# kv and kv Wo on TensorE: 32-column tiles in one batch, or 64-column tiles and four full matmuls

## The chip, the cores and the metric

The kernel runs on one core of one Trainium2 chip. The metric is the device time of one execution in microseconds. The kernel before took a median of 164.47 us over three runs (164.33 to 164.56).

## The reference, cut to what matters

The output mixes two branches of the same input `x` (2048 x 512, bf16), row by row, with a gate `g`:

```python
x = A_x
g = _sigmoid((x * gate_w).sum(-1, keepdims=True))
a = _A_ref(x, A_wqkv, A_wo)                 # linear attention, 32 heads of 16
b = _B_ref(x, B_w1, B_b1, B_w2, B_b2)       # layernorm, then an MLP over the tokens
return g * a + (1 - g) * b

# inside _A_ref; phi(t) = where(t > 0, t + 1, exp(t)) + 1e-6
pq, pk = phi(q), phi(k)
kv = jnp.einsum("bhsd,bhse->bhde", pk, v)
z = jnp.einsum("bhsd->bhd", pk)
num = jnp.einsum("bhqd,bhde->bhqe", pq, kv)
den = jnp.einsum("bhqd,bhd->bhq", pq, z)[..., None] + 1e-6
o = num / den                               # then put together and multiplied by wo
```

Per head, `kv` is a 16 x 16 matrix: the useful part of the 512 x 512 product of phi(k) and v is a chain of 32 diagonal blocks.

## The kernel before, in words

All engines run from one program written out by hand (`manual_schedule`): each engine executes its instructions in the order in which the code issues them. PSUM is one pool of eight banks with one tag, so a new bank waits for the readers of the one taken eight times earlier.

1. **k and G.** For each of 16 token tiles, `k_part` computes k in a bank, `k_phi` writes phi(k) to `pk`, and `g_tile`, four tiles later, accumulates `gacc` = x^T phi(k) in four banks. Copies put it in `gT`. The matrix v is never formed: kv is wv^T G for the diagonal blocks.
2. **q and the first MLP layer.** Three column blocks of u (`uacc`, 16 matmuls each, on the normalized input `hs`) are interleaved with 16 blocks of q, whose phi goes to `pqT`. `z_add` sums phi(k) over the token tiles, and `z_column` then turns the sum on VectorE into a column and spreads it by head into `Z32`.
3. **The rest of the first MLP layer.** The loop `for j in range(NB0, NF)` runs j = 3 to 13; each pass is 16 uacc matmuls and a gelu on ScalarE. Behind pass j = 6 stands a batch:
   - `kv_matmuls`: for each of four 128-wide column blocks `j` and four contraction blocks `k`, four matmuls of 128 rows x 32 columns, each at its own column tile of the array, so that only the 32-wide diagonal pieces are computed (64 matmuls, 32 columns streamed). One VectorE product with `maskQ` cuts the 16 x 16 heads out of them and writes `kvT` (L343).
   - `den_matmuls`: 16 matmuls of `Z32` with `pqT` at column tiles of 32, and the reciprocal `rden` on VectorE (L399).
   - `w2_matmuls`: kv times Wo in 16 matmuls of 32 x 32, over all 16 tile positions of the array, into four banks; position (i, i^j) means that a bank holds its four row groups in an order of its own.
   - `gate_sums` on VectorE, then `rden_chunk(0)` and `(1)`: the normalizer goes out to DRAM and comes back repeated over 16 rows (`rex`, GpSimd's queue), and VectorE multiplies `pqT` by it.

   `w2_copies` bring the banks to `W2sb` on ScalarE behind the gelus of j = 6 to 9; where the order of row groups differs they are copies of 32 or 64 rows, 11 in all (L386). `load_w2` loads the second MLP weights on SyncE's queue.
4. **Output.** For each of 16 token tiles: four matmuls `aps` = pqT x W2sb, 14 matmuls `yps`, ScalarE scales aps, VectorE joins them into `ot`, and SyncE stores it. `rden_chunk(2)` and `(3)` run during the first tiles.

Every matmul but the transposes is issued by the helper `mm`, so all have the line L113; the tiles' names tell them apart. In the code, `P` is 128, `ND` 4, `NQ` 4, `Q32` 32 and `HEAD` 16.

Of the kernel before, what the change touches and what calls it, by code (L numbers as in the profile page):

```python
# [7 lines left out]
ACT = mybir.ActivationFunctionType  # L8
ALU = mybir.AluOpType
AX = mybir.AxisListType  # L10
BF16 = mybir.dt.bfloat16
# [4 lines left out]
def kernel(  # L16
# [13 lines left out]
    nc = tc.nc  # L30
    P = nc.NUM_PARTITIONS
    EPS = 1e-5
    PHI_EPS = 1e-6
    HEAD = 16
# [6 lines left out]
    ND = D // P  # L41
# [5 lines left out]
    Q32 = 32  # L47
    NQ = P // Q32
# [18 lines left out]
    def keep(shape, dtype, name):  # L67
        return persist.tile(shape, dtype, name=name, tag=name)

    def bank(name, dtype=FP32):  # L70
        return ps.tile([P, SC], dtype, name=name, tag="bank")
# [6 lines left out]
    wv_sb = keep([P, ND, D], BF16, "wv_sb")  # L78
    wo_sb = keep([P, ND, D], BF16, "wo_sb")
    pqT = keep([P, ND, S], BF16, "pqT")  # L80
    pk = keep([P, NT, D], BF16, "pk")
    uT = keep([P, NF, D], BF16, "uT")
    kvT = keep([P, ND, Q32], BF16, "kvT")
    W2sb = keep([P, ND, D], BF16, "W2sb")
    Z32 = keep([P, ND * 40], BF16, "Z32")
    zacc = keep([P, D], FP32, "zacc")
# [4 lines left out]
    zcol = keep([P, ND], FP32, "zcol")  # L91
    rden = keep([P, SC], BF16, "rden")
    ident = keep([P, P], BF16, "ident")
    maskH = keep([P, 8], BF16, "maskH")
    maskQ = keep([P, 2], BF16, "maskQ")
    gw_b = keep([P, D], BF16, "gw_b")
    brow = keep([P, P], BF16, "brow")
    bcol = keep([P, NF + NT], FP32, "bcol")
# [13 lines left out]
    def mm(o, lhsT, rhs, start, stop, **kw):  # L112
        nc.tensor.matmul(o, lhsT=lhsT, rhs=rhs, start=start, stop=stop, **kw)  # L113

    def block_mask(m, cols, width):
        nc.gpsimd.memset(m, 1.0)
        nc.gpsimd.affine_select(
            out=m, in_=m, compare_op=ALU.is_ge, fill=0.0, base=0,
            pattern=[[-HEAD, cols], [0, width]], channel_multiplier=1,
        )  # L120
        nc.gpsimd.affine_select(
            out=m, in_=m, compare_op=ALU.is_ge, fill=0.0, base=HEAD - 1,
            pattern=[[HEAD, cols], [0, width]], channel_multiplier=-1,
        )
# [29 lines left out]
    for c, (j0, nb) in enumerate(w1_chunks):  # L154
        w = wpool.tile([P, NT, FB * P], BF16, name="w1c", tag="wc")
        w1c.append(w)
        for t0 in range(0, NT, 8) if c == 0 else (0,):
            t1 = t0 + 8 if c == 0 else NT
            nc.sync.dma_start(
                out=w[:, t0:t1, : nb * P], in_=w1_view[:, t0:t1, j0 * P : (j0 + nb) * P]  # L160
# [5 lines left out]
    nc.vector.memset(ones_f[:], 1.0)  # L166
    nc.vector.memset(mhalf[:], -0.5)
    nc.vector.memset(Z32[:], 0.0)
    nc.gpsimd.memset(ident[:], 0.0)
    nc.gpsimd.affine_select(  # L170
        out=ident[:], in_=ident[:], compare_op=ALU.not_equal, fill=1.0, base=0,
        pattern=[[-1, P]], channel_multiplier=1,
    )
    block_mask(maskH[:].rearrange("p (a b) -> p a b", b=1), 8, 1)

    nc.vector.tensor_reduce(
        out=maskQ[:], in_=maskH[:].rearrange("p (a m) -> p m a", m=2), op=ALU.max, axis=AX.X
    )
    nc.gpsimd.memset(brow[:], 0.0)

    def load_small():
# [134 lines left out]
    gT = persist.tile([P, ND, D], BF16, name="gT", tag="wk_sb")  # L316
# [6 lines left out]
    def gelu(j, acc):  # L323
        nc.scalar.activation(  # L324
            out=uT[:, j, :], in_=acc[:], func=ACT.Gelu_apprx_tanh, bias=bcol[:, j : j + 1]
        )

    def biases():
        pt = bank("pt", BF16)
        nc.tensor.transpose(pt[:, 0:P], brow[:], ident[:])  # L330
        nc.vector.tensor_copy(out=bcol[:], in_=pt[:, 0 : NF + NT])

    def kv_matmuls():
        kvps = bank("kvps")
        for j in range(ND):
            for k in range(ND):
                for q in range(0, P, Q32):
                    c = slice(j * P + q, j * P + q + Q32)
                    mm(
                        kvps[q : q + Q32, j * Q32 : (j + 1) * Q32], wv_sb[:, k, c], gT[:, k, c],  # L340
                        k == 0, k == ND - 1, tile_position=(0, q),
                    )
        nc.vector.tensor_tensor(  # L343
            out=kvT[:].rearrange("p j (m d) -> p j m d", d=HEAD),
            in0=kvps[:, 0 : ND * Q32].rearrange("p (j m d) -> p j m d", j=ND, d=HEAD),
            in1=maskQ[:].unsqueeze(1).unsqueeze(3).to_broadcast([P, ND, 2, HEAD]), op=ALU.mult,
        )

    def z_column():
        nc.vector.transpose(out=zT[:], in_=zacc[:])  # L350
# [16 lines left out]
            in1=maskH[:].unsqueeze(1).to_broadcast([P, ND, 8]), op=ALU.mult,  # L367
        )

    w2ps = []  # L370

    def w2_matmuls():
        w2ps.extend(bank("w2ps") for _ in range(ND))
        for j in range(ND):
            for i in range(NQ):
                r, c = i * Q32, (i ^ j) * Q32
                mm(
                    w2ps[j][c : c + Q32, :], kvT[r : r + Q32, j, :], wo_sb[r : r + Q32, j, :],
                    True, True, tile_position=(r, c),
                )  # L380

    def w2_copies(j):
        n = Q32 * (NQ, 1, 2, 1)[j]
        for r in range(0, P, n):
            c = (r // Q32 ^ j) * Q32
            nc.scalar.activation(  # L386
                out=W2sb[r : r + n, j, :], in_=w2ps[j][c : c + n, :], func=ACT.Copy
            )

    def den_matmuls():  # L390
        denps = bank("denps")
        for j in range(ND):
            for c in range(NSC):
                mm(
                    denps[32 * c : 32 * c + 32, :], Z32[:, 32 * j : 32 * j + 32], pqT[:, j, c * SC : (c + 1) * SC],
                    j == 0, j == ND - 1, tile_position=(0, 32 * c),
                )
        with nc.allow_low_precision(reason="the normalizer is used in bf16"):
            nc.vector.reciprocal(out=rden[:], in_=denps[:])  # L399

    NB0 = 3
# [21 lines left out]
    def gate_sums():  # L423
        for t in range(NT):
            junk = work.tile([P, D], BF16, name="junk", tag="junk", bufs=2)
            nc.vector.tensor_tensor_reduce(  # L426
                out=junk[:], in0=xs[:, t, :], in1=gw_b[:], scale=1.0, scalar=0.0,
                op0=ALU.mult, op1=ALU.add, accum_out=gpre[:, t : t + 1],
            )
# [3 lines left out]
    def rden_chunk(c):  # L433
        if c == 0:
            nc.gpsimd.dma_start(out=rd_dram[:], in_=rden[:])
        for j in range(ND):
            rex = work.tile([P, SC], BF16, name="rex", tag="rex", bufs=4)
            src = rd_dram[32 * c + 8 * j : 32 * c + 8 * j + 8, :]
            nc.gpsimd.dma_start(out=rex[:], in_=src.unsqueeze(1).to_broadcast([8, HEAD, SC]))  # L439
            seg = pqT[:, j, c * SC : (c + 1) * SC]  # L440
            nc.vector.tensor_tensor(out=seg, in0=seg, in1=rex[:], op=ALU.mult)  # L441
# [3 lines left out]
    def load_w2(c):  # L445
        w = wpool.tile([P, NT, FB * P], BF16, name="w2c", tag="wc")
        w2c.append(w)
        for f0 in (0, NF // 2):
            f1 = f0 + NF // 2
            nc.sync.dma_start(  # L450
                out=w[:, f0:f1, :], in_=w2_view[:, f0:f1, c * SC : (c + 1) * SC]
            )

    for j in range(NB0, NF):
        c, jj = divmod(j, FB)
        acc = bank("uacc")
        for t in range(NT):
            mm(acc[:], w1c[c][:, t, jj * P : (jj + 1) * P], hs[:, t, :], t == 0, t == NT - 1)
        gelu(j, acc)
        if j == NB0 + 3:  # L460
            kv_matmuls()
            den_matmuls()
            w2_matmuls()
            gate_sums()
            rden_chunk(0)
            rden_chunk(1)
        if NB0 + 3 <= j < NB0 + 3 + ND:
            w2_copies(j - NB0 - 3)
        if jj == FB - 1 or j == NF - 1:
            load_w2(c)  # L470

# [2 lines left out]
        out=gg[:], in0=gth[:], scalar1=0.5, scalar2=0.5, op0=ALU.mult, op1=ALU.add  # L474
    )
    nc.vector.tensor_scalar(
        out=c1[:], in0=gth[:], scalar1=-0.5, scalar2=0.5, op0=ALU.mult, op1=ALU.add
# [3 lines left out]
    for t in range(NT):  # L481
        c, tl = divmod(t, TPC)
        aps = bank("aps")
        for j in range(ND):
# [3 lines left out]
            out=a_sc[:], in_=aps[:], func=ACT.Identity,  # L488
            scale=gg[:, t : t + 1], bias=c2[:, t : t + 1],
        )  # L490
        for c0, W in ((0, D - P), (D - P, P)) if t == NT - 1 else ((0, D),):
            cs = slice(c0, c0 + W)
            yps = bank("yps")
            for f in range(NF):
# [6 lines left out]
                out=ot[:, :W], in0=yps[:, :W], scalar=c1[:, t : t + 1], in1=a_sc[:, cs],  # L501
# [35 lines left out]
```

## Time and profile before

| | us |
|---|---|
| median of three runs | 164.47 (164.33 to 164.56) |
| the profiled execution | 164.33 |
| its span, first to last instruction | 162.6 |
| TensorE (PE) busy | 158.0 |
| VectorE (DVE) busy | 89.5 |
| ScalarE (ACT) busy | 63.3 |
| GpSimd (POOL) busy | 17.5 |

The granted TensorE clock is 1.00 in the stages from 33 us on. In the rows, PE is the matmul and PEld the weight load beside it. A row of the timeline has the start, the duration, the engine, the line, the operation, the output and inputs, for a matmul the tile of the array (rows*columns) and the streamed operand, and the count; in brackets the idle time before it and what ended that. The start of a merged row is that of its first instruction. The chain in order of time has start, duration, engine, tile, line and count.

### The profile page before, as it was taken

How to read it: one execution, taken by the hardware profiler on the slowest of the kernel's cores; microseconds unless marked ns; L12 is line 12 of the kernel's file. 1: busy time of each engine (PE TensorE's matmuls, PEld its weight loads, DVE VectorE, ACT ScalarE, POOL GpSimd, SP SyncE). 2: the span in 40 equal slices, each digit the busy share in tenths (PEclk: the TensorE clock that was granted, in tenths of full speed). 3: DMA queues.
4: the chain of work that ended last, by engine and by line, in shares of the span. 5: the costliest groups of instructions: out<-in, count | busy, mean ns of one | idle time of the engine just before them, and what ended most of it. 6: DMA issues, size and time to landing. Idle time of an engine off the chain costs nothing.

```text
span 162.6 us, 2183 instructions
## 1 busy us (share of the span) xinstructions
PE 158.0 (97%) x823; PEld 72.9 (45%) x837; DVE 89.5 (55%) x210; ACT 63.3 (39%) x97; POOL 17.5 (11%) x34
## 2 busy tenths in 40 slices
PE   7999999999999999999999999999999999999992
PEld 2544444444444444444444444444444444444452
DVE  0599999967999999519995401166211111111112
ACT  3463386648667483212865113111122222111110
POOL 3000711200110000001415500050000000000000
PEclk9999999999999999999999999999999999999999
DMA  4999999999900006600892699732000001110001
GB/s 141 252 247 246 278 312 355 382 386 386 281 5 0 0 0 223 228 4 0 272 324 77 209 328 323 279 106 94 32 32 32 32 32 43 48 42 33 32 32 32
DMA packets 30057, 25.05 MB, mean 154 GB/s; under 512 B 7968, under 2 KB 29472, under 8 KB 30048
## 3 DMA queue, kind: packets, MB, share of 16 engines
q1 hardware_dynamic: 28032, 22.02, 42.9%
q0 software_dynamic: 1440, 2.38, 5.5%
q10 hardware_dynamic: 576, 0.52, 1.1%
q8 instruction: 6, 0.10, 0.2%
q14 instruction: 3, 0.02, 0.1%
HBM read 21.11 MB, written 2.23 MB: 144 GB/s over the span
## 4 chain that ended last, share of the span: by engine, by line
PE 96%; DMA 2%; issue 1%; DVE 0%
PE uacc L113 30%; PE yps L113 30%; PE kacc L113 9%; PE aps L113 8%; PE gacc L113 8%; PE qacc L113 8%; DMA xs<-in_A_x_dram 2%; PE pt L201 1%; PE denps L113 1%; PE kvps L113 0%; PE w2ps L113 0%; DVE ot L500 0%; PE pt L330 0%
## 5 line engine op out<-in xcount | busy, mean ns | idle before, releaser
L113 PE MATMUL uacc<-hs,w1c 128*128 128x512 bf16 x219 | 51.0, 379 | 0.4
L113 PE MATMUL yps<-uT,w2c 128*128 128x512 bf16 (+2 forms) x234 | 50.6, 366 | 0.2
L500 DVE SCALAR_TENSOR_TENSOR ot<-yps,c,a_sc 128x512 bf16<-128x512 f32 (+2 forms) x17 | 12.2, 719 | 44.8 <-PE yps L113 41.5
L113 PEld LDWEIGHTS <-w2c 128*128 128x128 bf16 x238 | 22.8, 98 | 25.9
L113 PEld LDWEIGHTS <-w1c 128*128 128x128 bf16 x224 | 21.8, 98 | 26.3 <-issue 0.2
L487 ACT ACTIVATE a_sc<-aps,c,gg 128x512 f32<-128x512 f32 x16 | 12.4, 777 | 46.7 <-PE aps L113 43.0
L324 ACT ACTIVATE uT<-uacc,bcol 128x512 bf16<-128x512 f32 x14 | 9.3, 688 | 21.7 <-PE uacc L113 21.7
L113 PE MATMUL aps<-W2sb,pqT 128*128 128x512 bf16 x63 | 16.2, 379 | 0.1
L113 PE MATMUL qacc<-xT,wq_sb 128*128 128x512 bf16 x63 | 16.2, 379 | 0.0
L113 PE MATMUL kacc<-wk_sb,xT 128*128 128x512 bf16 x63 | 16.1, 385 | 0.0
L113 PE MATMUL gacc<-pk,xs 128*128 128x512 bf16 x62 | 15.5, 379 | 0.1
L251 ACT ACTIVATE hs<-xs,nmr,rstd 128x512 bf16<-128x512 bf16 x16 | 12.8, 805 | 1.9 <-DVE nmr L245 1.9
L211 ACT ACTIVATE e<-qacc 128x512 bf16<-128x512 f32 x16 | 9.6, 597 | 9.2 <-PE qacc L113 8.3
L211 ACT ACTIVATE e<-kacc 128x512 bf16<-128x512 f32 x16 | 9.3, 595 | 6.9 <-PE kacc L113 5.6
L439 POOL DMA_DIRECT2D rex<-rd_dram x16 | 9.4, 598 | 22.9 <-DVE pqT L441 20.1
L215 DVE SCALAR_TENSOR_TENSOR pqT<-qacc,e 128x512 bf16<-128x512 f32 x16 | 11.1, 692 | 0.6
L215 DVE SCALAR_TENSOR_TENSOR pk<-kacc,e 128x512 bf16<-128x512 f32 x16 | 11.1, 692 | 0.6
L235 DVE BATCH_NORM_STATS2 stats<-xs 128x6 f32<-128x512 bf16 x16 | 10.9, 682 | 0.0
L212 DVE TENSOR_SCALAR e<-e 128x512 bf16<-128x512 bf16 x32 | 9.0, 282 | 3.2 <-ACT e L211 3.2
L426 DVE CUSTOM_DVE_ANT_0 junk<-xs,gw_b 128x512 bf16<-128x512 bf16 x16 | 9.8, 684 | 0.0
L276 DVE TENSOR_TENSOR zacc<-zacc,pk 128x512 f32<-128x512 f32 x14 | 9.6, 685 | 0.2
L113 PEld LDWEIGHTS <-pqT 128*128 128x128 bf16 x64 | 6.3, 98 | 7.6
(61 smaller groups left out, 71.7 us busy)
## 6 DMA issues: line engine op xcount, KB each, us to landing
w2c<-in_B_w_dram SPq DMA_DIRECT2D x8, 896.0 KB, 6.1
w1c<-in_B_w_dram SPq DMA_DIRECT2D x2, 2048.0 KB, 14.7
w1c<-in_B_w_dram SPq DMA_DIRECT2D x3, 1024.0 KB, 11.9
rex<-rd_dram POOLq DMA_DIRECT2D x16, 128.0 KB, 4.0
out_dram<-ot SPq DMA_DIRECT2D x15, 128.0 KB, 1.7
xs<-in_A_x_dram SPq DMA_DIRECT2D x3, 512.0 KB, 4.4
wq_sb<-in_A_wqkv_dram SPq DMA_DIRECT2D x1, 512.0 KB, 6.3
wv_sb<-in_A_wqkv_dram SPq DMA_DIRECT2D x1, 512.0 KB, 11.8
```

The source lines that it names most:

```text
L113: nc.tensor.matmul(o, lhsT=lhsT, rhs=rhs, start=start, stop=stop, **kw)
L211: nc.scalar.activation(out=e[:], in_=acc[:], func=ACT.Exp)
L212: nc.vector.tensor_scalar(out=e[:], in0=e[:], scalar1=1.0, scalar2=PHI_EPS, op0=ALU.min, op1=ALU.add)
L215: nc.vector.scalar_tensor_tensor(out=dst, in0=acc[:], scalar=0.0, in1=e[:], op0=ALU.max, op1=ALU.add)
L235: nc.vector.bn_stats(out=stats[:], in_=xs[:, t, :])
L251: nc.scalar.activation(out=hs[:, t, :], in_=xs[:, t, :], func=ACT.Identity, scale=rstd[:, t : t + 1], bias=nmr[:, t : t + 1],)
L276: nc.vector.tensor_tensor(out=zacc[:], in0=first, in1=pk[:, t, :], op=ALU.add)
L324: nc.scalar.activation(out=uT[:, j, :], in_=acc[:], func=ACT.Gelu_apprx_tanh, bias=bcol[:, j : j + 1])
L426: nc.vector.tensor_tensor_reduce(out=junk[:], in0=xs[:, t, :], in1=gw_b[:], scale=1.0, scalar=0.0, op0=ALU.mult, op1=ALU.add, accum_out=gp ...
L439: nc.gpsimd.dma_start(out=rex[:], in_=src.unsqueeze(1).to_broadcast([8, HEAD, SC]))
L487: nc.scalar.activation(out=a_sc[:], in_=aps[:], func=ACT.Identity, scale=gg[:, t : t + 1], bias=c2[:, t : t + 1],)
L500: nc.vector.scalar_tensor_tensor(out=ot[:, :W], in0=yps[:, :W], scalar=c1[:, t : t + 1], in1=a_sc[:, cs], op0=ALU.mult, op1=ALU.add,)
```

## The change

kv is computed in column tiles of 64 instead of 32 (two diagonal pieces of 64 for each 128-wide block), so there are 32 matmuls instead of 64, each streaming 64 columns. Two VectorE products with a 128 x 128 mask, one for each half of the partitions, write the 16 x 16 blocks into `kvbdT`, which holds a block-diagonal 128 x 128 matrix for each of four column blocks and is cleared at the start. kv times Wo becomes four full 128 x 128 matmuls of 512 columns, each with one full copy on ScalarE; they leave the batch behind j = 6 and stand one each behind the passes j = 8 to 11. The column of sums (`z_column`) and `den_matmuls` are the same in both. At the start the small `maskQ` and its VectorE reduction go, and the mask on GpSimd and the clearing of `kvbdT` on VectorE come.

```diff
-    kvT = keep([P, ND, Q32], BF16, "kvT")
+    kvbdT = keep([P, ND, P], BF16, "kvbdT")
...
+    mask = keep([P, P], BF16, "mask")
     maskH = keep([P, 8], BF16, "maskH")
-    maskQ = keep([P, 2], BF16, "maskQ")
...
     nc.vector.memset(Z32[:], 0.0)
+    nc.vector.memset(kvbdT[:], 0.0)
...
+    block_mask(mask[:].rearrange("p (a b) -> p a b", b=HEAD), P // HEAD, HEAD)
     block_mask(maskH[:].rearrange("p (a b) -> p a b", b=1), 8, 1)
 
-    nc.vector.tensor_reduce(
-        out=maskQ[:], in_=maskH[:].rearrange("p (a m) -> p m a", m=2), op=ALU.max, axis=AX.X
-    )
...
+    H2 = P // 2
+
     def kv_matmuls():
         kvps = bank("kvps")
         for j in range(ND):
             for k in range(ND):
-                for q in range(0, P, Q32):
-                    c = slice(j * P + q, j * P + q + Q32)
+                for h in (0, H2):
+                    c = slice(j * P + h, j * P + h + H2)
                     mm(
-                        kvps[q : q + Q32, j * Q32 : (j + 1) * Q32], wv_sb[:, k, c], gT[:, k, c],
-                        k == 0, k == ND - 1, tile_position=(0, q),
+                        kvps[h : h + H2, c], wv_sb[:, k, c], gT[:, k, c], k == 0, k == ND - 1,
+                        tile_position=(0, h),
                     )
-        nc.vector.tensor_tensor(
-            out=kvT[:].rearrange("p j (m d) -> p j m d", d=HEAD),
-            in0=kvps[:, 0 : ND * Q32].rearrange("p (j m d) -> p j m d", j=ND, d=HEAD),
-            in1=maskQ[:].unsqueeze(1).unsqueeze(3).to_broadcast([P, ND, 2, HEAD]), op=ALU.mult,
-        )
+        for h in (0, H2):
+            d = slice(h, h + H2)
+            nc.vector.tensor_tensor(
+                out=kvbdT[d, :, d],
+                in0=kvps[d, :].rearrange("p (j d) -> p j d", j=ND)[:, :, d],
+                in1=mask[d, d].unsqueeze(1).to_broadcast([H2, ND, H2]), op=ALU.mult,
+            )
...
-    w2ps = []
-
-    def w2_matmuls():
...
-    def w2_copies(j):
...
+    def w2_matmul(j):
+        wps2 = bank("wps2")
+        mm(wps2[:], kvbdT[:, j, :], wo_sb[:, j, :], True, True)
+        nc.scalar.activation(out=W2sb[:, j, :], in_=wps2[:], func=ACT.Copy)
...
             kv_matmuls()
             den_matmuls()
-            w2_matmuls()
             gate_sums()
             rden_chunk(0)
             rden_chunk(1)
-        if NB0 + 3 <= j < NB0 + 3 + ND:
-            w2_copies(j - NB0 - 3)
+        if NB0 + 5 <= j < NB0 + 5 + ND:
+            w2_matmul(j - NB0 - 5)
```

More of the change, by code (lines that the diff above doesn't have):

```diff
@@ L368, in z_column @@
         )
-    w2ps = []
-    def w2_matmuls():
[L373 to L380, printed above, removed]
-    def w2_copies(j):
[L383 to L388, printed above, removed]
+    def w2_matmul(j):
+        wps2 = bank("wps2")
+        mm(wps2[:], kvbdT[:, j, :], wo_sb[:, j, :], True, True)
+        nc.scalar.activation(out=W2sb[:, j, :], in_=wps2[:], func=ACT.Copy)
     def den_matmuls():
```

## The prediction

> **What bounds the kernel now.** I read the page first, its busy times and the chain of waits, then the chain in order of time around the changed lines, then the timeline of the same stretch.
>
> ```profile
> PE 158.0 (97%) x823; PEld 72.9 (45%) x837; DVE 89.5 (55%) x210; ACT 63.3 (39%) x97; POOL 17.5 (11%) x34
> PE 96%; DMA 2%; issue 1%; DVE 0%
> ```
>
> TensorE is busy for 97% of the span and makes 96% of the chain that ends last. So a change counts by the TensorE time it adds or takes, and work of other engines counts only where it stops TensorE. The chain in order of time shows the changed stretch and the price of ordinary matmuls:
>
> ```profile
> 6.83 0.22 PE pt L201 x4
> ...
> 71.42 0.59 PE kvps L113 x64
> 72.02 0.88 PE denps L113 x16
> 72.90 0.36 PE w2ps L113 x16
> 73.26 0.32 PE uacc L113
> ...
> 98.41 3.02 PE yps L113 x14
> ```
>
> The last row gives a 128x512 matmul in a dense stream: 3.02 / 14 = 0.2157 us. The first gives a 128x128 one with a fresh full weight load each: 0.22 / 4 = 0.055 us. Of the three changed rows denps stays as it is. The chain's pieces follow modelled ends; I cost the stretch from start to start, by the timeline:
>
> ```profile
> 71.05 0.38 PE L113 MATMUL uacc<-hs,w1c 128*128 128x512 bf16 x1
> 71.36 0.66 PE L113 MATMUL kvps<-gT,wv_sb 128*32 128x32 bf16 x64
> 71.84 1.06 PE L113 MATMUL denps<-pqT,Z 128*32 128x512 bf16 x16
> 72.11 0.29 DVE L343 TENSOR_TENSOR kvT<-kvps,maskQ 128x128 bf16<-128x128 f32 x1 [4.67 <-PE kvps L113]
> 72.83 0.43 PE L113 MATMUL w2ps<-wo_sb,kvT 32*32 32x512 bf16 x16
> 72.94 3.36 DVE L399 RECIPROCAL rden<-denps 128x512 bf16<-128x512 f32 x1 [0.54 <-PE denps L113]
> 73.19 1.04 PE L113 MATMUL uacc<-hs,w1c 128*128 128x512 bf16 x3
> ```
>
> (The first row is the answer for a narrow window, so that the last uacc matmul before the batch stands alone.) From its start at 71.05 to the next uacc at 73.19 pass 2.14 us, in four steps: 0.31 to the first kvps, 0.48 for 64 kvps, 0.99 for 16 denps, 0.36 for 16 w2ps. Where the tile shape changes (128x128 to 128x32, 128x32 to 32x32, back to 128x128) the next start comes about 0.31 after the last one instead of 0.216: a switch costs 0.095 us. From kvps to denps, both 128x32, no such gap shows. The w2ps gap isn't kvT's doing: kvT is done at 72.40, 0.43 us earlier.
>
> The pace within kvps comes from windows that end at different times:
>
> ```profile
> 71.36 0.27 PE L113 MATMUL kvps<-gT,wv_sb 128*32 128x32 bf16 x14
> 71.36 0.37 PE L113 MATMUL kvps<-gT,wv_sb 128*32 128x32 bf16 x30
> 71.36 0.47 PE L113 MATMUL kvps<-gT,wv_sb 128*32 128x32 bf16 x41
> 71.36 0.57 PE L113 MATMUL kvps<-gT,wv_sb 128*32 128x32 bf16 x53
> ```
>
> They are the counts started by 71.45, 71.55, 71.65 and 71.75. At first 16 start in 0.10 us, so the four column tiles run beside each other at 25 ns a round; later 12 in 0.10 us, 8.3 ns each, which looks like the rate at which matmuls with their loads are issued.
>
> **The change, part by part.**
>
> *kv.* 64 matmuls of 128x32 tiles become 32 of 128x64 tiles, two beside each other, 64 columns streamed: 16 rounds. No row has a 64-column tile. Between 128 columns (55 ns) and 512 (215.7) the slope is 0.418 ns a column, so 64 columns come to 55 - 64 x 0.418 = 28 ns; the floor from kvps is 25 ns, and issue (2 x 8.3 = 17 ns a round) is under both. The bounds are 25 ns (narrow weight loads hidden, as in kvps) and 55 ns (the 128-column row, all 128 weight columns of a round loaded at its price). I take 28, since kvps shows the loads of a round hidden. From first to last round: 15 x 28 = 0.42 us.
>
> Here a page speaks against the change. The Trainium skill, "TensorE: Matmul & The Clock Gate", section "LDWEIGHTS (loading the stationary operand)", puts a load at its columns divided by 1.2 ns, 53 ns for 64 columns, and "Weight-path perf modes" keeps the faster load for full 128-column weights. By that a round would take 53 ns and the whole sum below 0.38 us more. The row of kvps, 25 ns, already lies under the 27 ns that the rule gives for 32 columns, so I leave the rule to the upper end.
>
> *kv to den.* The shapes now differ (128x64, then 128x32), so a switch appears there: 28 + 95 = 0.12 us to the first denps; low end, no switch, 0.03. In return the one between denps and w2ps goes: the next instruction is an ordinary uacc, at the same 0.31.
>
> *den.* Unchanged: 0.99 - 0.31 = 0.68 us from first to last.
>
> *kv Wo.* The 16 packed matmuls (0.36 us with the switch behind them) go; four 128x128 matmuls of 512 columns come, one each behind the uacc groups j = 8 to 11: 4 x 0.2157 = 0.86 us. They have the shape of the stream around them, so no switch. What they wait for is early: kvbdT is ready some 6 us before the first one, and PSUM banks come round after eight uses, behind readers that ended microseconds before.
>
> *Sum, start to start.* 0.31 + 0.42 + 0.12 + 0.68 + 0.31 + 0.86 = 2.70 us against 2.14: 0.56 us longer.
>
> *VectorE.* One masking copy of 0.29 us becomes two of 64 partitions x 256 elements. From 128 elements (292 ns) and the 512-element copies out of PSUM (692 ns, pk and pqT) the slope is 1.04 ns, so 0.43 us each, 0.85 together. Queued behind them are the reciprocal, the gate sums and the pqT products. kvps would end near 71.36 + 0.42 + 0.18 = 71.96, VectorE pick up near 72.06 and be done at 72.91; denps, started at 71.90, ends at 71.90 + 0.68 + 0.38 = 72.96. So the reciprocal still starts with denps' end, at about 73.0 instead of 72.94. Without that cover it would start 0.56 later, and that would cost nothing either: the products of chunk 0 end at 88.0 in this trace, and TensorE reads them at 97.4.
>
> *ScalarE.* Eleven W2sb copies (6.5 us) become four full ones (0.60 each, 2.4 us). TensorE waits for none of them now; the last would end near 92.5 and be read at about 98.5. The gain is bounded by TensorE's slack in that stretch: 112 uacc matmuls from 73.19 to 97.38 take 24.19 us against 112 x 0.2157 = 24.16. So 0.03 us at most.
>
> *Start.* GpSimd makes the 128x128 mask (0.20 for a memset and twice 0.29, by ident's rows) ahead of maskH and brow, VectorE clears kvbdT (0.12 for a row a third as wide; some 0.3) and no longer waits for maskH until 2.06. All that ends near 3.0 us, while TensorE waits for xs until 3.7 and VectorE's first copy starts at 4.38; ident itself is made before the mask. The small loads on GpSimd's queue come after 10 us. Uncovered, it would cost under 1 us; it is covered, so nothing. SyncE's queue has no instruction moved.
>
> **Against the clock.** The profiled execution took 164.33 us, with 162.6 of span and 1.7 around it; the sum gives 164.33 + 0.56 = 164.89 for it. The median of the runs is 0.14 above it, 164.47, so I predict 165.03.
>
> **Rivals.**
> 1. *Weight loads set the kv pace.* At 55 ns a round: 15 x 55 = 0.83, and 0.15 to denps, so 3.14 against 2.14, +1.00: 165.47. For it: narrow tiles may not load like full ones, and the later part of kvps is slower than its first. Against it: 25 ns a round for 128 weight columns in four tiles. Two loads in series, 110 ns a round, would be +1.9, 166.3; I see nothing for that.
> 2. *Not slower: the batch is issue-bound, and fewer instructions repay W2.* If kv is paced by issue alone (32 x 8.3 = 0.27 us) and 128x64 to 128x32 needs no switch, the sum is 0.31 + 0.27 + 0.68 + 0.31 + 0.86 = 2.43, +0.29: 164.76, within 0.33 us of before. It decides once kv with its way to denps takes 0.31 us or less. For it: the late rounds of kvps are at just that rate. Against it: 64 columns cost 28 ns a round by the slope, not 17, and shapes that change have switched at all three places so far.
> 3. *Faster.* W2's four matmuls would have to fall into idle TensorE time, but the stretch has 0.03 us of it; even case 2 is above zero. Only a gain elsewhere, of over 0.9 us beside a loss of 0.56, would do, and no row holds one.
>
> **How the numbers follow.** 0.2% is 0.33 us, about what a measurement of this kernel tells from no change. The main case (28 ns a round, a switch) has 0.62, rival 1 has 0.24, rival 2 0.10, rival 3 0.04. The main case and rival 1 are slower by over 0.33 us, but for 0.01 of the main case with a low measurement: slower 0.85, same 0.11, faster 0.04. The low end takes 25 ns and no switch (2.56, +0.42, 164.89) less the 0.2 by which runs of one kernel differ here: 164.7. The high end is rival 1 with 0.1 for the same: 165.6.
>
> **What would show it.** Right: kvps with 32 matmuls, some 0.55 us from its first start to the first denps; a gap there of about 0.1 us over a round; W2 matmuls at 0.216 us within the uacc stream, nothing waiting around them; 2.70 us for the changed parts together; later stages the same length, only shifted. Wrong: over 0.9 us from kvps to denps (rival 1), under 0.35 (rival 2), a hole before a W2 matmul or the first aps, or a reciprocal so late that pqT products hold up the output stage.

## The result and the profile after

The changed kernel took a median of 165.33 us (165.09 to 165.48, six runs) against 164.50 us (163.88 to 164.69, six runs) for the kernel before: a ratio of 1.0055, 95% interval 1.0037 to 1.0073, so slower: by 0.83 us between the medians, by 0.9 us by the ratio. The forecast was 165.03 us in a range of 164.7 to 165.6. The profiled execution took 165.22 us with a span of 163.4.

The stretch around the batch, from the timeline of the changed kernel (the first row is again the answer for a narrow window):

```profile
71.20 0.38 PE L113 MATMUL uacc<-hs,w1c 128*128 128x512 bf16 x1
71.51 0.69 PE L113 MATMUL kvps<-gT,wv_sb 128*64 128x64 bf16 x32
72.13 1.05 PE L113 MATMUL denps<-pqT,Z 128*32 128x512 bf16 x16
72.24 0.86 DVE L346 TENSOR_TENSOR kvbdT<-kvps,mask 64x256 bf16<-64x256 f32 x2 [4.66 <-PE kvps L113]
73.11 0.39 PE L113 MATMUL uacc<-hs,w1c 128*128 128x512 bf16 x1
73.23 3.36 DVE L387 RECIPROCAL rden<-denps 128x512 bf16<-128x512 f32 x1
```

From start to start: 0.31 us to the first kvps, 0.62 for 32 kvps, 0.98 for denps with the switch back, 1.91 together. Then the chain in order of time, with the W2 matmuls (here `wps`) inside the uacc stream:

```profile
80.19 0.22 PE wps L113
80.41 3.45 PE uacc L113 x16
83.86 0.22 PE wps L113
...
87.53 0.22 PE wps L113
87.75 3.45 PE uacc L113 x16
91.20 0.22 PE wps L113
```

Each adds 0.22 us and nothing stands idle beside it. From the first uacc behind the batch to the first aps pass 25.05 us (73.11 to 98.16), against 24.19 before: 0.86 more. So the changed parts take 1.91 + 0.86 = 2.77 us instead of 2.14, 0.63 us more on TensorE. Of the 0.89 us between the two profiled executions, 0.15 lie ahead of the first gacc matmul (it starts at 9.91 us before, at 10.06 after), 0.63 in the changed parts and 0.11 outside the span. Over all runs the time outside the span grew more. What lies behind the span shows in the DMA view of a window from 162 to 167 us. First the kernel before, then the changed one:

```profile
q14 instruction: 1, 0.01, 0.4%
```

```profile
q14 instruction: 2, 0.02, 1.0%
```

The columns are packets, MB and share. These are code fetches, of 8192 bytes each in the trace. The trace of the kernel before has one at 163.2 us, 0.6 us behind its span; the changed one has two, at 163.7 and 165.2. The second starts 1.81 us behind the span, and the time outside the span of that execution is 1.85 us. Over all runs the time outside the span (time less span) was 1.73 us in the kernel before and 1.88 in the changed one.

### The profile page after: what moved, and what is told of

Read it like the earlier page. It is cut to its first block, busy times and chain, and to the rows that moved or that the text cites. A ratio compares the mean times of both kernels' runs of the same rounds, so it can differ in the third digit from the quotient of the medians.

```text
span 163.4 us, 2092 instructions
## 1 busy us (share of the span) xinstructions
PE 158.9 (97%) x779; PEld 73.2 (45%) x793; DVE 90.1 (55%) x211; ACT 58.7 (36%) x90; POOL 18.3 (11%) x37
## 2 busy tenths in 40 slices
DMA packets 30057, 25.05 MB, mean 153 GB/s; under 512 B 7968, under 2 KB 29472, under 8 KB 30048
## 4 chain that ended last, share of the span: by engine, by line
PE 97%; issue 1%; DVE 0%
PE uacc L113 30%; PE yps L113 29%; PE kacc L113 9%; PE aps L113 9%; PE gacc L113 8%; PE qacc L113 8%; PE wps L113 2%; PE pt L200 1%; PE denps L113 1%; PE kvps L113 0%; DVE ot L487 0%; PE pt L329 0%
## 5 line engine op out<-in xcount | busy, mean ns | idle before, releaser
L113 PE MATMUL uacc<-hs,w1c 128*128 128x512 bf16 x219 | 51.7, 379 | 0.4
L113 PEld LDWEIGHTS <-xT 128*128 128x128 bf16 x64 | 6.4, 100 | 7.6 <-ACT xT L204 0.4
```

## The experiments

Each kernel was built on the changed one or on the one before and timed against the latter on the same chip. "Batch" is the time from the last uacc start ahead of kvps to the first uacc start behind the batch, plus 4 x 0.216 where the four full W2 matmuls stand elsewhere: 2.15 us before and 2.78 changed from the unrounded starts in the traces, where the rows above, rounded to 0.01 us, give 2.14 and 2.77. "Outside" is the mean of time less span over all runs of a kernel.

| kernel | batch, us | outside, us | fetches behind the span | ratio (95% interval) |
|---|---|---|---|---|
| before | 2.15 | 1.73 to 1.74 | 1 | |
| changed | 2.78 | 1.88 | 2 | 1.0055 (1.0037 to 1.0073) |
| e1: kv32, W2 full | 2.65 | 1.95 | 2 | 1.0048 (1.0032 to 1.0065) |
| e2: kv64, W2 packed | 2.28 | 1.73 | 1 | 1.0008 (0.9995 to 1.0021) |
| e3: W2 in the batch | 2.84 | 1.97 | 2 | 1.0060 (1.0039 to 1.0081) |
| e4: start as before | 2.78 | 1.92 | 2 | 1.0058 (1.0038 to 1.0078) |
| e5: mask on VectorE | 2.78 | 1.72 | 1 | 1.0055 (1.0036 to 1.0074) |
| e6: before, 3 GpSimd more | 2.15 | 1.90 | 2 | 1.0015 (1.0000 to 1.0030) |
| e9: a denps round first | 2.17 | 1.79 | 1 | 0.9989 (0.9977 to 1.0000) |
| e10: before, other layout | 2.15 | 1.72 | 1 | 1.0000 (0.9990 to 1.0009) |
| e11: changed, again | 2.78 | 1.96 | 2 | 1.0047 (1.0033 to 1.0061) |

e7 and e8 were executed once each (165.53 and 166.0 us) and are read in the trace alone.

### Which half of the change costs (e1, e2)

e1, on the changed kernel:

```diff
-                for h in (0, H2):
-                    c = slice(j * P + h, j * P + h + H2)
+                for q in range(0, P, Q32):
+                    c = slice(j * P + q, j * P + q + Q32)
                     mm(
-                        kvps[h : h + H2, c], wv_sb[:, k, c], gT[:, k, c], k == 0, k == ND - 1,
-                        tile_position=(0, h),
+                        kvps[q : q + Q32, j * Q32 : (j + 1) * Q32], wv_sb[:, k, c], gT[:, k, c],
+                        k == 0, k == ND - 1, tile_position=(0, q),
                     )
...
```

(The masking product is split into four to match.)

> The changed kernel with one part undone: kv again in 64 matmuls of 128x32 tiles (four masking copies of 32 partitions write kvbdT), W2 still in four full matmuls. Theory (the extra time is TensorE time, nearly all of it W2): last uacc to next uacc around the batch 0.31 + 0.48 + 0.68 + 0.31 = 1.78 us, plus 4 x 0.216 = 0.86, so 2.64 against 2.14 before: +0.50 us, or 0.13 us less than the changed kernel. Rival (the 64-column kv carries the loss): the time comes back to within 0.2 us of before.

The timeline of e1:

```profile
71.26 0.38 PE L113 MATMUL uacc<-hs,w1c 128*128 128x512 bf16 x1
71.57 0.66 PE L113 MATMUL kvps<-gT,wv_sb 128*32 128x32 bf16 x64
72.05 1.06 PE L113 MATMUL denps<-pqT,Z 128*32 128x512 bf16 x16
73.04 0.39 PE L113 MATMUL uacc<-hs,w1c 128*128 128x512 bf16 x1
```

From uacc to uacc are 1.78 us; the four full W2 matmuls add 0.86 (2.65 in all, unrounded).

e2, on the kernel before:

```diff
+    H2 = P // 2
...
-                for q in range(0, P, Q32):
-                    c = slice(j * P + q, j * P + q + Q32)
+                for h in (0, H2):
+                    c = slice(j * P + h, j * P + h + H2)
                     mm(
-                        kvps[q : q + Q32, j * Q32 : (j + 1) * Q32], wv_sb[:, k, c], gT[:, k, c],
-                        k == 0, k == ND - 1, tile_position=(0, q),
+                        kvps[h : h + H2, j * H2 : (j + 1) * H2], wv_sb[:, k, c], gT[:, k, c],
+                        k == 0, k == ND - 1, tile_position=(0, h),
                     )
```

> The kernel before with one part of the change: kv in 32 matmuls of 128x64 tiles, W2 still packed in 16 tile positions. The masking product reads the first 128 columns of the bank as before, not the diagonal pieces, so kvT doesn't hold the reference's kv; only the time is read. Theory: 0.31 + 0.50 + 0.125 + 0.67 + 0.31 + 0.36 = 2.27 us around the batch against 2.14: +0.13 us, near the bound of what the times tell. Rival (64-column kv carries the loss): +0.4 us or more.

The timeline of e2:

```profile
71.33 0.38 PE L113 MATMUL uacc<-hs,w1c 128*128 128x512 bf16 x1
71.64 0.69 PE L113 MATMUL kvps<-gT,wv_sb 128*64 128x64 bf16 x32
72.27 1.05 PE L113 MATMUL denps<-pqT,Z 128*32 128x512 bf16 x16
73.24 0.43 PE L113 MATMUL w2ps<-wo_sb,kvT 32*32 32x512 bf16 x16
73.61 0.39 PE L113 MATMUL uacc<-hs,w1c 128*128 128x512 bf16 x1
```

The step from kvps to denps is 0.63 us, as in the changed kernel, and the steps behind it are those of the kernel before. On TensorE the two halves add up: +0.13 us (2.28 - 2.15) for the wider kv tiles, +0.50 (2.65 - 2.15) for the full W2, 0.63 together. The rival, that kv carries the loss, falls. The times did not add up so well: e1 lost 0.8 us where its batch explains 0.5, and 0.22 of the rest is time outside the span (1.95 against 1.73). e2 lost just its 0.13, which its interval does not tell from nothing; there the trace decides.

### Whether the place of W2 matters (e3)

```diff
             den_matmuls()
+            for jw in range(ND):
+                w2_matmul(jw)
...
-        if NB0 + 5 <= j < NB0 + 5 + ND:
-            w2_matmul(j - NB0 - 5)
```

> The changed kernel with the four full W2 matmuls put back into the batch, right behind denps, instead of behind the passes j = 8 to 11. Theory (their price is their streaming alone, wherever they stand): the first W2 starts about 0.31 us behind the last denps or up to 0.1 us later, for kvbdT, which is ready near the same time; the kernel takes 0 to 0.1 us more than the changed one. Rival (standing between uacc groups costs something, a bank or a copy on ScalarE): the kernel is 0.2 us or more faster than the changed one.

```profile
72.18 1.05 PE L113 MATMUL denps<-pqT,Z 128*32 128x512 bf16 x16
72.29 0.86 DVE L346 TENSOR_TENSOR kvbdT<-kvps,mask 64x256 bf16<-64x256 f32 x2 [4.66 <-PE kvps L113]
73.21 1.04 PE L113 MATMUL wps<-wo_sb,kvbdT 128*128 128x512 bf16 x4
74.08 0.38 PE L113 MATMUL uacc<-hs,w1c 128*128 128x512 bf16 x1
```

From denps to the next shape are 1.03 us instead of 0.98: the four matmuls waited 0.05 us for kvbdT, which VectorE had ready at 73.15. Then they stream for 0.87 us. The kernel is not faster than the changed one (ratio 1.0060 against 1.0055), so the rival falls. The place costs nothing; spreading them only takes this small wait away.

### The start (e4)

```diff
-    nc.vector.memset(kvbdT[:], 0.0)
...
-    block_mask(mask[:].rearrange("p (a b) -> p a b", b=HEAD), P // HEAD, HEAD)
...
+    nc.vector.memset(kvbdT[:], 0.0)
+    block_mask(mask[:].rearrange("p (a b) -> p a b", b=HEAD), P // HEAD, HEAD)
     z_column()
```

> The changed kernel with its start as in the kernel before: the mask on GpSimd and the clearing of kvbdT are moved to just ahead of z_column, far from the start. The changed kernel's profile lies 0.15 us behind the one before already at 11 us, where the rise of the TensorE clock came at 6.2 instead of 5.7 us. Theory (the rise falls where it falls, whatever the change): the time stays within 0.15 us of the changed kernel, and in the profiles of these four kernels the rise moves by some tenths without regard to what they do at the start. Rival (the longer start delays it): rise at 5.7 us here and in the run with W2 packed, 6.2 in the two others, and about 0.25 us less than the changed kernel.

With the old start the kernel takes 165.32 us, the same as the changed one. In the traces the TensorE clock rises at 3.9 us (e1), 6.4 (e2), 4.4 (e3) and 4.5 (e4), without regard to the start: the rival falls. (From the rise on, matmuls of one shape start about half as far apart, in e1 those of 128 columns 56 ns instead of 107; the kernel before has it at 5.7 us, the changed one at 6.2.) Nor does the first stage follow the rise: the first gacc matmul starts at 10.12 us in e1 and at 9.91 in the kernel before. The Trainium skill ("TensorE: Matmul & The Clock Gate", "Part 1: The HAM clock gate") says that the activity window runs freely and so meets a kernel's start at any phase, and gives 500 ns to either side for the point of the rise. That the rise comes at no fixed point agrees; the spread over all traces here, 3.9 to 6.8 us, is wider than that figure, and the measurement decides.

### The time behind the span (e5, e6)

All kernels with the full W2 up to here had two fetches behind the span and 0.15 to 0.24 us more outside it. They differ from the others by three GpSimd instructions more (the mask), and seven ScalarE instructions fewer. e5, on the changed kernel:

```diff
-    block_mask(mask[:].rearrange("p (a b) -> p a b", b=HEAD), P // HEAD, HEAD)
...
+    nc.vector.tensor_copy(
+        out=mask[:].rearrange("p (a b) -> p a b", b=HEAD),
+        in_=maskH[:].unsqueeze(2).to_broadcast([P, P // HEAD, HEAD]),
+    )
```

> The changed kernel with its 128x128 mask spread from maskH by one VectorE copy at the start, instead of three GpSimd instructions. So GpSimd has as many instructions as in the kernel before, ScalarE stays at seven fewer. What it is for: the changed kernel, and every kernel with four full W2 matmuls so far, spends 1.88 to 1.97 us outside its span where the kernel before spends 1.73, and shows two 8 KB instruction fetches behind the end of the span where the kernel before shows one. Theory (GpSimd's three more instructions push its last code into another block): one fetch behind the span, 1.73 us outside it, and 0.15 to 0.2 us less than the changed kernel. Rival (ScalarE's seven fewer, or VectorE's, shift their blocks): two fetches, 1.9 us outside, time as the changed kernel.

e6, on the kernel before:

```diff
+    mask = keep([P, P], BF16, "mask")
...
+    block_mask(mask[:].rearrange("p (a b) -> p a b", b=HEAD), P // HEAD, HEAD)
     block_mask(maskH[:].rearrange("p (a b) -> p a b", b=1), 8, 1)
```

> The kernel before with the three GpSimd instructions of the changed kernel's mask added at the start; nothing reads that mask. Theory (GpSimd's count): two fetches behind the span, some 1.9 us outside it, and 0.15 to 0.2 us more than the kernel before, with TensorE's work the same. Rival (ScalarE's or VectorE's count): one fetch, 1.73 us, no difference.

The DMA view of the same window, first for e5, then for e6:

```profile
q14 instruction: 1, 0.01, 0.6%
```

```profile
q14 instruction: 2, 0.02, 1.3%
```

In the fetches and in the time outside the span both went as the theory has it: without the three GpSimd instructions the changed kernel has one fetch and 1.72 us outside; with them the kernel before has two and 1.90, with the same TensorE work. e6 adds nothing but the GpSimd instructions. So these, not ScalarE's, bring the second fetch and 0.16 to 0.18 us outside the span.

The whole times show it less clearly. e6 takes 0.15% more, with an interval that begins at zero. One part of the expectation for e5 failed: its median, 165.28, is only 0.05 us under the changed kernel's, for its spans were longer (163.50 us on average against 163.43, though e5 also has one VectorE copy more at the start).

The Trainium skill ("Runtime: NRT & Kernel Launch", "Instruction fetch mechanics") has code fetched in blocks as an engine goes, a crossing mostly hidden. No run here prices the fetches within the span. That a block edge is what the three instructions cross is inferred from the fetch that comes with them, not seen. Nor is it shown that the time waits for this fetch: in the changed kernel's trace it starts only 0.04 us before the time outside the span is over (1.81 of 1.85 us; 0.23 us before it in e6's), if all of that time lies behind the span.

### What sets the pace of the 64-column tiles (e7, e8)

e7 streams `gT[:, k, c.start : c.start + 32]`, e8 all 128 columns `gT[:, k, j * P : (j + 1) * P]`, with the same 128x64 tiles of weights.

> The changed kernel with only the first 32 of 64 columns streamed in each kv matmul, the tiles still 128x64 (half of the kv blocks is left out, so only the pace is read). In the changed kernel a round of two 64-column tiles takes 31.4 ns, where I had put 28. If the streamed columns set that, a round comes down to the 25 ns seen for 32 columns; if the 64 weight columns set it, it stays at 31.

> The changed kernel with 128 columns streamed in each kv matmul, the tiles still 128x64; the additional columns are not used. If the streamed columns set the pace, a round takes 55 ns, as a 128-column matmul with a full load does, and kv from first to last start 0.83 us instead of 0.47; if load and stream added up it would be near 60 or more.

The starts in the traces give 31 to 32 ns a round for 64 streamed columns, the same for 32 (e7), and 55 to 56 for 128 (e8). The timeline of e7, then of e8:

```profile
71.81 0.68 PE L113 MATMUL kvps<-gT,wv_sb 128*64 128x32 bf16 x32
72.42 1.05 PE L113 MATMUL denps<-pqT,Z 128*32 128x512 bf16 x16
```

```profile
71.86 1.08 PE L113 MATMUL kvps<-gT,wv_sb 128*64 128x128 bf16 x32
72.87 1.05 PE L113 MATMUL denps<-pqT,Z 128*32 128x512 bf16 x16
```

Halving the stream leaves the 0.62 us at 0.61; doubling it brings the pace to that of a 128-column matmul. So the pace is the longer of two things: the stream, or some 31.5 ns that do not depend on it. The 8.3 ns between late kvps starts make only 17 ns a round, so what is left for the 31.5 is the load of two tiles of 64 weight columns beside each other; in the traces of the changed kernel and of e7 the pairs of loads start 28 to 32 ns apart. This is reached by exclusion: no run changes the load alone (e7 has wider tiles than the kernel before, but also two a round instead of four). The first round alone takes 52 ns (80 in e8), perhaps because the second pair of loads is not ahead of the matmuls there; that is not tested. The rule of 53 ns for every load of 64 columns, weighed in the prediction, is not borne out.

### A try at a better kernel (e9)

```diff
-            den_matmuls()
+            den_matmuls((0,))
+            kv_matmuls()
+            den_matmuls((1, 2, 3))
```

(`den_matmuls` takes the column blocks that it computes; `kv_matmuls()` stood first. maskH and brow are made on VectorE.)

> A try at a kernel better than both: the kernel before with the first of four denps rounds put ahead of kv, and with maskH taken from ident by one VectorE reduction and brow cleared on VectorE (four GpSimd instructions fewer). First part: in the kernel before the last 28 kvps matmuls start 8.3 ns apart, at the rate of issue; behind a denps round of 0.216 us more of them should be queued and go at 25 ns for four, so kvps takes 0.40 to 0.42 us instead of 0.48 and the batch 2.07 instead of 2.15. If issue is no limit there, nothing changes. Second part: if four fewer GpSimd instructions bring its last code back over one more block edge, the fetch behind the span goes and the time outside it falls under 1.73 us; if the edge is further away, as I think likelier, both stay. Together -0.08 us, under what the times can tell, so it is read in the trace.

```profile
71.21 0.40 PE L113 MATMUL denps<-pqT,Z 128*32 128x512 bf16 x4
71.43 0.67 PE L113 MATMUL kvps<-gT,wv_sb 128*32 128x32 bf16 x64
71.93 0.84 PE L113 MATMUL denps<-pqT,Z 128*32 128x512 bf16 x12
```

kvps takes 0.50 us, no less: 28 matmuls come fast, 36 in the kernel before, and the others 8.3 ns apart in both. So a longer wait ahead does not queue more of them, and what sets the 8.3 ns stays open. The batch is 0.02 us longer (2.17 against 2.15). The fetch behind the span stays too. The time came out 0.11% under the kernel before, at the edge of its interval, with spans 0.25 us shorter. Nothing in the batch or outside the span explains this. The start was changed too, and the first gacc matmul is the earliest of all traces (9.76 us), but one trace does not tell this from the scatter of the start (below), so I don't call the kernel better.

### What is left (e10, e11)

e10 adds unused tiles `pad` and `mpad` to the kernel before, cleared at the start; e11 is the changed kernel unaltered.

> The kernel before with two unused tiles beside kvT and maskQ, as large as what kvbdT and the mask add, cleared on VectorE at the start, so that the tiles behind them lie in SBUF where the changed kernel has them. The changed kernels' mean span exceeds that of the kernel before by about 0.1 us more than their batch and W2 explain. Theory (it is the scatter of the start, some 0.25 us from one execution to the next): mean span within 0.08 us of the kernel before. Rival (place in SBUF or the clearing at the start delays the first stage): 0.1 us or more above it.

> The changed kernel again, unaltered, beside the two others on the same chip. Theory (0.63 us of TensorE, 0.17 us of the fetch behind the span, the rest scatter): 0.80 us over the kernel before, within 0.15. Rival (a further 0.1 to 0.15 us in the start is the change's own): 0.90 to 0.95.

e10's mean span is 162.82 us against 162.78 before: no cost of the layout or the clearing shows. e11 is 0.77 us over the kernel before (0.0047 x 164.56), near the 0.80 of 0.63 + 0.17; its interval, 0.54 to 1.00, holds the rival's 0.90 to 0.95 as well. What is left is in the first stage: the first gacc matmul starts at 9.91 us in the profile of the kernel before, at 10.06 and 9.96 in the two of the changed one, between 9.76 (e9) and 10.41 (e8) in all. In e6 and e10, which are the kernel before but for some instructions at the start, it is at 10.25 and 10.23, later than in both traces of the changed kernel. From there to the first kvps nothing differs (61.45 us, but for the denps round in e9). Mean spans less batches lie between 160.36 us (e9) and 160.73 (e5). Whether 0.1 us of it belongs to the changed kernels was not settled.

## Why the prediction was right, and where it was off

- **The bound and the sum.** TensorE sets the time, and the sum from start to start held: 0.63 us measured for 0.56 (2.78 us less 2.15, where I had 2.70 less 2.14). Rival 2 (not slower) needed kvps and its way to denps in 0.31 us; it took 0.62. Rival 1 needed 0.98.
- **kv: the mis-sized term.** I put 0.42 us for the 15 rounds, 28 ns each, from the slope of streamed columns. It is 0.50: the first round takes 52 ns and the others 31.5, whether 64 or 32 columns are streamed (e7). So the streamed columns, from which I took the price, do not set it, and I was wrong that the loads of a round are hidden, if the load is what is left. The 31.5 lies nearer to my 28 than to the 53 of the rule. (At 53 a round the sum would have been 0.40 us more, with the step to denps, not 0.38.)
- **The switches.** As predicted: 0.125 us from the last kvps to denps, and none between denps and uacc beyond the 0.31 already there.
- **kv Wo.** 0.86 predicted, 0.86 measured; nothing waits; put into the batch the four take the same 0.87, behind a wait of 0.05 for kvbdT (e3).
- **VectorE and ScalarE.** Two masking products of 0.86 together (0.85 predicted); the reciprocal starts 1.72 us behind the first kvps instead of 1.58, and TensorE does not notice: from the first uacc behind the batch to the first aps it takes 24.19 us before and 24.19 + 0.86 after. The last W2sb copy ends near 92.4 us.
- **The start: the step that failed.** I wrote that GpSimd's three instructions cost nothing, as other work covers them. At the start this is so (e4). But they bring one more fetch behind the span and 0.17 us more outside it (e5, e6), where the prediction had left the 1.7 us around the span as they were. I costed the instructions' execution and not their presence in the program. How they lengthen that time is inferred, not seen.

The two errors, 0.07 and 0.17 us, take 0.56 to 0.80; the repeat gave 0.77, the first measurement 0.83 to 0.9. That the time lay within the range is partly luck: its high end was put there for slow weight loads (rival 1), not for anything outside the span.

## What to carry to other kernels

Small matmuls packed over the tile positions of the array can be cheap even with the shape switch that they add: 16 of them cost 0.36 us here where four full ones cost 0.86. Widening a column tile did not pay: half as many matmuls, with twice the weight columns each, took 0.13 us more. Cost a dense TensorE stream from start to start, and for narrow tiles price the weight load beside the stream and take the longer. Compare the time outside the span as well as the span: three instructions that were hidden when they ran came with 0.17 us outside it.

## What I had not expected of the hardware

- A round of two 64-column tiles side by side takes 31.5 ns, whether 64 or 32 columns are streamed; a round of four 32-column tiles with 32 streamed takes 25.
- After the first 36 matmuls of 32-column tiles the others start 8.3 ns apart, and a 0.216 us round of other work ahead of them does not bring more of them through fast (28 in e9).
- Three instructions on GpSimd, far off the critical path, came with 0.17 us more outside the span (e5, e6).
